# Sliding-window attention with a token mixer: 192 score columns per head and key block, query blocks shifted by 64

## The chip, the cores and the metric

The kernel runs on one core of one Trainium2 chip. The metric is the device time of one execution in microseconds, lower is better. The kernel before took 135.03, 134.73 and 133.62 us in three executions, median 134.73 us.

## What is computed

Attention with a window of 128 keys and a linear distance bias, for 8 batches, 8 heads, 576 positions and head size 64; then a token mixer without a softmax on the 512 joined head columns.

```python
scores = q @ k.T / sqrt(64)                       # B=8, H=8, S=576, D=64
rel    = pos[:, None] - pos[None, :]
mask   = (rel >= 0) & (rel < 128)
scores = where(mask, scores - slope[h] * abs(rel), -1e9)
x      = softmax(scores) @ v                      # joined over heads: [B, 576, 512]
W      = (x @ w_q) @ (x @ w_k).T / sqrt(64)       # w_q, w_k: [512, 64]
out    = relu(W @ x) @ w_out                      # w_out: [512, 512], float32 out
```

A query sees itself and the 127 positions before it. Equally, a key is seen by the 128 queries that begin at its own position.

## The kernel before

**Order of the work.** The program is a graph of small operations, each with its dependencies (`Op`, `Graph.add`). The order in which each engine issues them is written out by hand in one string, ORDER (lines 35 to 119). A word such as `QK2.1.0@PE:2` gives the operation, its engine and its PSUM bank pair (two digits name one bank of a pair); `+11` puts eleven filler matmuls ahead of it. Every engine takes its words strictly in that order, so a word that has to wait holds all later words of its engine. Some PSUM evacuations may stand on ScalarE (ACT) or VectorE (DVE), as the string says.

**Loads.** q, k and v come in by DMAs issued on POOL, one for each block of 128 positions of a batch (Lq, Lk, Lv), with a cast to f16; the last 64 positions of two batches share a load (Lt, Lv with part 4). The first half of batch 0 comes in two loads on SP (Lf). Weights are Lw (w_q, w_k) and Lwo. All of them go through `load` (line 379, the DMA at 383). The buffers hold four batches.

**Attention.** TQ and TT transpose q and k on PE by 64x128 pieces, two row halves (two heads) at a time; ETQ and ETT copy the result to SBUF. For a batch b and a key block g of 128 keys, QK (lines 526 to 548) makes the scores of four heads (u is 0 or 1) with the keys on the partitions and 256 queries in the columns, those from the block's first key on. It is four matmuls, two at a time on two row halves. Key block 3 has 192 such queries, and its last 64 columns take the tail: the last 64 keys with the last 64 queries. EXP (556) makes the exponential of 1024 columns on ACT. MUL (566) multiplies 2048 columns, eight heads, on DVE with a table `bias` that holds the exponential of the distance bias, zero outside the window; `biasl` is the table for block 3. PV (571 to 606) multiplies the result with v, to which a column of ones is joined, so that column 64 of each head is the softmax sum. A query block of 128 takes two key blocks (blocks 1 to 3) or one (block 0), one matmul per head and key block on the full array; part 4 is the tails of two batches on tiles of 64 columns. X (613, 614) takes the reciprocal and scales on DVE.

**Mixer.** XT and EXT transpose x. WQ (669) multiplies x with w_q, which is held twice side by side so that the result stands in both partition halves; EWQ copies it. WK (695 to 701) multiplies x with w_k so that the positions stand on the partitions: four matmuls for each of five blocks of positions; EWK copies it. G sums (x w_k) against x over the positions, MX multiplies the result with x w_q, RM applies ReLU, OUT multiplies with w_out, EO copies to SBUF, DO stores. Up to 26 such output tiles are held in SBUF (HELD). The stores of batches 0 to 5 are issued on POOL behind all loads (lines 850 and 851), those of 6 and 7 on SP.

In the profile most PE work has line 228 (`mm`) or 231 (`tp`, transposes), copies have 235, 237, 241 or 243, so operations are told apart by their tiles: `qkT` QK, `vt,pt` PV, `wk_sb,xT` WK, `xT,wqq_sb` WQ, `x,wkn` G, `wqT,gs` MX, `wout_sb,rm` OUT, `identh,nat` TQ, `identh,natt` TT, `identh,x` XT. The shape of the array (128\*128, 64\*128, 128\*64) stands behind them: rows by columns of one tile.

Of the kernel before, what the change touches and what calls it, by code (L numbers as in the profile page):

```python
# [14 lines left out]
P = 128  # L15
# [12 lines left out]
NPT = 6  # L28
HELD = 26
# [6 lines left out]
zeros@DVE iota@POOL Lf1.0@SP pads@POOL dist@DVE mask@DVE Lf0.0@SP ident@POOL ones2@DVE bias0@ACT  # L36
Lh0.1@POOL idh@DVE ones0@DVE Lh1.1@POOL bias1@ACT Lt0.1@POOL C1.0.1@DVE C1.0.0@ACT Lq1.3@POOL
C0.0.1@ACT biasl1@DVE TQ0.0.1@PE:0+11 C0.0.0@ACT Lk1.3@POOL ETQ0.0.1.0@DVE ETQ0.0.1.1@ACT
TQ0.0.0@PE:1+3 Lt0.0@POOL ETQ0.0.0.1@DVE ETQ0.0.0.0@ACT C0.1.0@ACT ones3@DVE QK0.0.0@PE:0+3/20
Lk1.1@POOL biasl0@DVE QK0.2.0@PE:1 QK0.1.0@PE:2 EXP0.0.0@ACT TQ0.1.0@PE:3 Lk1.2@POOL ETQ0.1.0.0@DVE  # L40
C1.1.0@ACT ETQ0.1.0.1@DVE Lq1.2@POOL EXP0.2.0@ACT TQ0.1.1@PE:0+1 ETQ0.1.1.0@DVE Lk1.0@POOL
EXP0.1.0@ACT ones1@DVE QK0.1.1@PE:1+2/30 ETQ0.1.1.1@DVE QK0.0.1@PE:3 Lq1.1@POOL EXP0.1.1@ACT
QK0.2.1@PE:0+1 TT0@PE:2 Lq1.0@POOL EXP0.2.1@ACT ETT0@DVE ETT1@DVE QK0.3.1@PE:1+1 Lv0.0@POOL
MUL0.1@DVE QK0.3.0@PE:2 EXP0.0.1@ACT Lv0.1@POOL EXP0.3.0@ACT MUL0.2@DVE TQ1.2@PE:0+5 Lw0@POOL
Lv0.2@POOL ETQ1.2@ACT MUL0.0@DVE Lv0.3@POOL EXP0.3.1@ACT QK1.3.1@PE:0+6/30 QK1.3.0@PE:2 QK1.2.0@PE:3
Lk2.0@POOL EXP1.3.1@ACT TQ1.0@PE:1 MUL0.3@DVE Lv0.4@POOL ETQ1.0@ACT PV0.0@PE:0 Lq2.0@POOL X0.0@DVE
EXP1.3.0@ACT PV0.1@PE:1 wqq@DVE Lv1.3@POOL QK1.1.1@PE:0 MUL1.3@DVE QK1.1.0@PE:2 EXP1.1.1@ACT
Lq2.1@POOL EXP1.1.0@ACT X0.1@DVE PV0.2@PE:0 Lv1.2@POOL X0.2@DVE EXP1.2.0@ACT Lw1@POOL QK1.0.0@PE:1
QK1.2.1@PE:2 Lk2.1@POOL MUL1.1@DVE EXP1.2.1@ACT PV0.3@PE:0 Lv1.1@POOL XT0.0@PE:3 EXP1.0.0@ACT
MUL1.2@DVE QK1.0.1@PE:2 Lv1.0@POOL EXT0.0@ACT PV0.4@PE:1 X0.3@DVE Lk2.3@POOL EXP1.0.1@ACT  # L50
WQ0.0@PE:30 X0.4@DVE Lq2.2@POOL XT0.1@PE:0 PV1.3@PE:2 EXT0.1@ACT MUL1.0@DVE Lk2.2@POOL XT0.2@PE:31
XT1.2@PE:10 TQ2.0@PE:0 EXT0.2@ACT EXT1.2@ACT Lq2.3@POOL WK0@PE:31 EWQ0.0@DVE ETQ2.0@ACT X1.3@DVE
PV1.2@PE:1 Lk3.2@POOL WQ0.1@PE:30 EWK0@ACT X1.2@DVE PV1.0@PE:0 Lwo0@POOL EWQ0.1@ACT QK2.0.1@PE:2
X1.0@DVE Lwo3@POOL PV1.1@PE:1 EXP2.0.1@ACT Lwo2@POOL QK2.0.0@PE:3 X1.1@DVE G0@PE:00 EXP2.0.0@ACT
Lwo1@POOL XT1.1@PE:2 EG0@DVE Lt2.1@POOL XT1.0@PE:1 EXT1.1@ACT MUL2.0@DVE MX0.0@PE:0 MX0.1@PE:3
EXT1.0@ACT Lv2.0@POOL TQ2.2@PE:2 RM0.0@ACT WQ1.0@PE:10 ETQ2.2@DVE Lt2.0@POOL WQ1.1@PE:11 RM0.1@ACT
WK1@PE:00 Lq3.0@POOL EWQ1.1@DVE QK2.2.0@PE:2 EWQ1.0@DVE EWK1@ACT QK2.2.1@PE:3 Lq3.3@POOL
EXP2.2.0@ACT MX0.4@PE:1 G1@PE:00 RM0.4@DVE Lk3.3@POOL OUT0.3@PE:01 EXP2.2.1@ACT EG1@DVE Lq3.2@POOL
MX1.4@PE:1 QK2.1.1@PE:2 EO0.3@DVE MX1.1@PE:3 RM1.4@ACT EXP2.1.1@ACT Lk3.0@POOL OUT0.1@PE:00
RM1.1@DVE Lq3.1@POOL TT2@PE:1 EO0.1@ACT QK2.1.0@PE:2 MUL2.2@DVE MX1.0@PE:3 EXP2.1.0@ACT Lk3.1@POOL  # L60
OUT1.4@PE:01 ETT2@DVE RM1.0@ACT Lk4.1@POOL OUT0.0@PE:00 ETT3@DVE MUL2.1@DVE Lv2.1@POOL QK2.3.1@PE:2
EO0.0@ACT QK2.3.0@PE:1 TQ3.2@PE:3 EXP2.3.1@ACT EO1.4@DVE Lv2.4@POOL OUT1.1@PE:00 ETQ3.2@DVE
EXP2.3.0@ACT Lv2.3@POOL PV2.0@PE:2 OUT1.2@PE:01 X2.0@DVE Lv3.3@POOL EO1.1@ACT QK3.3.1@PE:3 EO1.2@ACT
MUL2.3@DVE Lv2.2@POOL TQ3.0@PE:1 EXP3.3.1@ACT QK3.3.0@PE:2 OUT1.3@PE:00 Lq4.0@POOL ETQ3.0@DVE
EXP3.3.0@ACT PV2.1@PE:3 Lk4.0@POOL EO1.3@ACT QK3.1.1@PE:1 X2.1@DVE QK3.1.0@PE:2 Lq4.1@POOL
EXP3.1.1@ACT OUT0.2@PE:01 MUL3.3@DVE Lv3.1@POOL EXP3.1.0@ACT XT2.0@PE:3 QK3.0.1@PE:1 Lq4.2@POOL
EXT2.0@DVE OUT1.0@PE:00 EXP3.0.1@ACT MUL3.1@DVE Lk4.3@POOL PV2.2@PE:2 EO0.2@ACT QK3.2.0@PE:3
Lq4.3@POOL EO1.0@ACT X2.2@DVE PV2.3@PE:1 EXP3.2.0@ACT QK3.2.1@PE:0 Lv3.2@POOL X2.3@DVE PV2.4@PE:2
EXP3.2.1@ACT TQ4.0@PE:3 Lk4.2@POOL X2.4@DVE XT2.1@PE:1 ETQ4.0@ACT WQ2.0@PE:00 Lk5.2@POOL EXT2.1@DVE
XT2.2@PE:01 QK3.0.0@PE:2 EWQ2.0@DVE XT3.2@PE:10 Lv3.0@POOL EXT2.2@ACT QK4.0.0@PE:3 MUL3.2@DVE  # L70
EXP3.0.0@ACT WK2@PE:11 Lt4.1@POOL WQ2.1@PE:00 EXP4.0.0@ACT EWK2@DVE QK4.0.1@PE:2 MUL3.0@DVE
Lk5.3@POOL G2@PE:01 EWQ2.1@ACT EXP4.0.1@ACT Lq5.3@POOL PV3.2@PE:3 EG2@DVE MX2.1@PE:0 X3.2@DVE
EXT3.2@ACT Lq5.2@POOL MX2.0@PE:2 RM2.1@ACT TQ4.2@PE:1 RM2.0@DVE Lq6.3@POOL PV3.3@PE:3 ETQ4.2@ACT
OUT2.3@PE:00 Lt4.0@POOL X3.3@DVE PV3.0@PE:2 EO2.3@ACT QK4.2.0@PE:1 Lv4.1@POOL X3.0@DVE PV3.1@PE:3
EXP4.2.0@ACT Lv4.0@POOL QK4.2.1@PE:0 X3.1@DVE OUT2.0@PE:20 EXP4.2.1@ACT Lq5.1@POOL MUL4.0@DVE
XT3.0@PE:1 EO2.0@ACT QK4.1.1@PE:3 Lk5.1@POOL XT3.1@PE:0 EXT3.0@ACT OUT2.2@PE:21 EXT3.1@DVE
EXP4.1.1@ACT Lq5.0@POOL MUL4.2@DVE QK4.1.0@PE:1 TT4@PE:0 EO2.2@ACT Lk5.0@POOL TQ5.2@PE:3
EXP4.1.0@ACT ETT4@DVE WQ3.1@PE:20 ETQ5.2@DVE Lv4.2@POOL WK3@PE:21 ETT5@ACT EWQ3.1@ACT Lk6.1@POOL
QK4.3.1@PE:1 MUL4.1@DVE EWK3@ACT QK4.3.0@PE:0 MX2.4@PE:3 EXP4.3.1@ACT G3@PE:20 Lv4.3@POOL RM2.4@DVE
WQ3.0@PE:21 EXP4.3.0@ACT Lq6.0@POOL EG3@DVE PV4.0@PE:1 EWQ3.0@DVE MX3.1@PE:3 X4.0@DVE PV4.1@PE:2  # L80
Lq6.2@POOL RM3.1@ACT MX3.0@PE:0 X4.1@DVE TQ5.0@PE:1 Lq6.1@POOL RM3.0@ACT QK5.3.1@PE:3 ETQ5.0@DVE
OUT2.1@PE:20 Lv4.4@POOL EXP5.3.1@ACT Lv5.3@POOL QK5.3.0@PE:0 EO2.1@DVE XT4.0@PE:1 EXP5.3.0@ACT
QK5.0.0@PE:3 EXT4.0@DVE OUT3.1@PE:21 Lk6.0@POOL MUL4.3@DVE EXP5.0.0@ACT Lk6.2@POOL QK5.2.0@PE:1
# [83 lines left out]
def kernel(  # L167
# [51 lines left out]
    def two(bank):  # L219
        return pairs[bank[0]]  # L220

    held = []

    def hold(i):
        held.append(i.ins)

    def mm(*a, **k):
        hold(nc.tensor.matmul(*a, **k))  # L228

    def tp(*a):  # L230
        hold(nc.tensor.transpose(*a))  # L231

# [658 lines left out]
```

## Time and profile before

| | |
|---|---|
| three executions | 133.62, 134.73, 135.03 us |
| span of the profiled execution, first to last instruction | 132.4 us |
| mean granted TensorE clock | 0.997 |
| PE, DVE, ACT, POOL busy | 121.7, 112.3, 112.9, 109.6 us |
| PE busy in 0 to 30 us | 10.00 of 10: 8.09, 8.43, 7.54 |
| HBM read, written | 29.62 MB, 9.44 MB |

The executions in the first row include what lies around the span. In the profile an operation's duration is its own, while successive matmuls overlap: the distance from one start to the next says what PE spends, not the sum of durations. A row of PE's timeline merges matmuls of the same tiles that follow one another.

### The profile page before, as it was taken

Reading aid. Unit: us, or ns where it says so; the run is one execution under the profiler, and the core shown is the slowest. Engines: PE = TensorE matmul, PEld = TensorE weight load, DVE = VectorE, ACT = ScalarE, POOL = GpSimd, SP = SyncE. Lnnn points to the kernel's source line nnn. Section 1 sums busy time; section 2 is a strip of 40 time slices with the busy share of each in tenths; the row PEclk is TensorE's granted clock in tenths of the full one; section 3 lists DMA queues with packets and bytes.
Section 4 is the critical chain, followed back from the end, with each engine's and each line's share of the span. In section 5 each row is a group of like instructions: output and inputs, shape, how many; then the busy total and the mean of one; then the engine's idle time right before and its main releaser. Section 6 shows DMA issues by size and latency. Waiting matters only on the chain.

```text
span 132.4 us, 5423 instructions
## 1 busy us (share of the span) xinstructions
PE 121.7 (92%) x2349; PEld 77.6 (59%) x2349; DVE 112.3 (85%) x206; ACT 112.9 (85%) x163; POOL 109.6 (83%) x147
## 2 busy tenths in 40 slices
PE   6988795888999999999999999999999999999970
PEld 2343364676774565767677667567567656863430
DVE  6776958997978999999999999999999999982530
ACT  5999779986999999999999999999999897554730
POOL 7999879999999999999999999999968509790000
PEclk9999999999999999999999999999999999999998
DMA  3999999999999999999999999999999936999775
GB/s 119 275 148 155 157 158 152 149 151 149 189 156 158 156 155 153 157 153 154 156 154 156 153 152 153 156 157 152 157 212 376 374 125 228 334 303 367 285 211 185
DMA packets 110663, 25.12 MB, mean 190 GB/s; under 512 B 104816, under 2 KB 107888, under 8 KB 110640
## 3 DMA queue, kind: packets, MB, share of 16 engines
q0 software_dynamic: 108128, 21.37, 178.4%
q1 hardware_dynamic: 2512, 3.41, 7.5%
q8 instruction: 18, 0.29, 0.8%
q14 instruction: 5, 0.04, 0.1%
HBM read 29.62 MB, written 9.44 MB: 295 GB/s over the span
## 4 chain that ended last, share of the span: by engine, by line
PE 77%; ACT 7%; POOL 6%; DMA 6%; issue 1%; POOLq 0%; ACTq 0%
PE pair L228 67%; PE pair L231 10%; DMA nat<-in_q_dram 6%; ACT pt L556 5%; POOL nat L383 4%; ACT qkT L241 1%; POOL natt L383 1%; ACT osb L235 1%; POOL ident masks.py:199 0%; POOL ident masks.py:197 0%; POOL xT L339 0%; POOL xT L340 0%; POOL wint L311 0%; ACTq L556 0%; POOLq L311 0%
## 5 line engine op out<-in xcount | busy, mean ns | idle before, releaser
L556 ACT ACTIVATE pt<-pair 128x1024 f16<-128x1024 f32 x64 | 63.2, 1033 | 1.6 <-PE pair L228 1.3
L383 POOL DMA_DIRECT2D vt<-in_v_dram x32 | 31.7, 1138 | 0.9 <-DMA nat<-in_q_dram 0.9
L228 PE MATMUL pair<-wout_sb,rm 128*128 128x512 f16 (+1 forms) x132 | 32.4, 374 | 0.0
L383 POOL DMA_DIRECT2D nat<-in_k_dram x29 | 29.2, 1059 | 0.5 <-DVE pt L566 0.5
L383 POOL DMA_DIRECT2D nat<-in_q_dram x29 | 29.0, 1058 | 0.1
L566 DVE TENSOR_TENSOR pt<-pt,bias 128x2048 f16<-128x2048 f16 x24 | 29.0, 1217 | 0.0
L228 PE MATMUL pair<-vt,pt 128*128 128x65 f16 (+1 forms) x512 | 21.4, 194 | 2.9 <-ACT pt L556 1.6
L228 PE MATMUL pair<-qkT 64*128 64x256 f16 (+2 forms) x320 | 23.3, 250 | 0.8 <-DVE qkT L243 0.3
L228 PEld LDWEIGHTS <-pt 128*128 128x128 f16 (+1 forms) x576 | 19.0, 100 | 8.1 <-issue 6.0
L614 DVE TENSOR_TENSOR x<-pair,inv 128x512 f16<-128x512 f32 x32 | 22.1, 692 | 1.1
L235 ACT COPY osb<-pair 128x512 f32<-128x512 f32 (+1 forms) x29 | 16.7, 585 | 4.3 <-PE pair L228 4.0
L797 POOL DMA_DIRECT2D out_dram<-osb x24 | 13.5, 604 | 6.4 <-ACT osb L235 4.7
L228 PEld LDWEIGHTS <-rm 128*128 128x128 f16 x132 | 10.9, 97 | 11.9 <-issue 1.9
L228 PEld LDWEIGHTS <-qkT 64*128 64x128 f16 x320 | 10.8, 94 | 8.3 <-issue 4.7
L731 ACT ACTIVATE rm<-pair 128x1024 f16<-128x1024 f32 (+1 forms) x12 | 11.3, 956 | 1.4 <-PE pair L228 1.2
L228 PE MATMUL pair<-fill 128*128 128x512 f16 x33 | 10.6, 453 | 1.7 <-DVE fill L364 1.2
L243 DVE COPY qkT<-pair 128x2048 f16<-128x2048 f16 (+1 forms) x12 | 10.4, 884 | 1.5 <-PE pair L231 1.5
L231 PEld LDWEIGHTS <-nat 64*128 64x128 f16 x512 | 9.1, 95 | 4.0 <-ACT nat L235 1.3
L231 PE MATMUL pair<-identh,nat 64*128 64x64 f16 x512 | 10.4, 190 | 1.1 <-DMA nat<-in_q_dram 0.7
L566 DVE TENSOR_TENSOR pt<-pt,biasl 128x2048 f16<-128x2048 f16 x8 | 9.7, 1219 | 1.6 <-ACT pt L556 1.6
L228 PE MATMUL pair<-xT,wqq_sb 128*128 128x256 f16 (+1 forms) x64 | 10.4, 287 | 0.0
L241 ACT COPY qkT<-pair 128x1024 f32<-128x1024 f32 (+1 forms) x10 | 8.2, 834 | 1.5 <-PE pair L231 1.4
(66 smaller groups left out, 161.8 us busy)
## 6 DMA issues: line engine op xcount, KB each, us to landing
out_dram<-osb POOLq DMA_DIRECT2D x24, 256.0 KB, 4.7
vt<-in_v_dram POOLq DMA_DIRECT2D x32, 128.0 KB, 6.0
nat<-in_q_dram POOLq DMA_DIRECT2D x28, 128.0 KB, 5.7
nat<-in_k_dram POOLq DMA_DIRECT2D x28, 128.0 KB, 5.8
out_dram<-osb SPq DMA_DIRECT2D x7, 256.0 KB, 2.6
out_dram<-osb POOLq DMA_DIRECT2D x6, 128.0 KB, 4.3
nat<-in_k_dram SPq DMA_DIRECT2D x1, 512.0 KB, 3.8
nat<-in_q_dram SPq DMA_DIRECT2D x1, 512.0 KB, 4.7
```

The costliest lines, as they stand in the source:

```text
L228: hold(nc.tensor.matmul(*a, **k))
L231: hold(nc.tensor.transpose(*a))
L235: hold(nc.scalar.copy(out_ap, in_ap))
L241: hold(nc.scalar.copy(out_ap.bitcast(FP32), in_ap.bitcast(FP32)))
L243: hold(nc.vector.tensor_copy(out=out_ap, in_=in_ap))
L383: op = add(kind, b, part, (eng,), deps, lambda o: q.dma_start(out=dst, in_=src), size=size)
L556: nc.scalar.activation(out=pt[:, u, 0:1024], in_=two(s.bank).rearrange("p e c -> p (e c)"), func=AF.Exp, scale=SCALE)
L566: nc.vector.tensor_tensor(out=pt[:, :, 0:1024], in0=pt[:, :, 0:1024], in1=bt, op=ALU.mult)
L614: nc.vector.tensor_tensor(out=x.rearrange("p (g h d) -> p g h d", g=2, h=4), in0=pxv[:, :, :, 0:64], in1=inv.unsqueeze(3).broadcast_to([P, ...
L731: hold(nc.scalar.activation(out=out_ap, in_=in_ap, func=AF.Relu, scale=WSCALE))
L797: q.dma_start(out=out[b, P * st:P * st + P, c], in_=osb)
```

## The change

**Scores by half key blocks.** A key block of 128 keys is treated as two halves of 64. Each half needs the 191 queries that begin at its own first key, so 192 columns serve it (KW). The scores of the lower half stand in PSUM partitions 0 to 63, for queries 128g to 128g+191. Those of the upper half stand in partitions 64 to 127: columns 64 to 191 are queries 128g+64 to 128g+191, columns 0 to 63 are the next 64 queries (in block 3: the tail keys and queries). So columns 64 to 191 have the same queries in both halves, and columns 0 to 63 have other queries in each. EXP covers 768 columns, MUL 1536. A QK unit is twelve matmuls on 64x64 tiles.

**Query blocks shifted by 64.** Block qt now covers queries 64+128qt to 64+128qt+127, the tail block the first 64 queries of two batches. PV gives the main product: one key block, columns 64 to 191, full array. The side products come from columns 0 to 63 on 64x64 tiles: the lower key half of block qt+1 for the block's upper 64 queries, the upper key half of block qt-1 for its lower 64 (PW; in blocks 1 and 2 PS and PW). PS and PW of one query block write the two PSUM banks crosswise from two row halves. Between them stands T, an empty instruction on SP that waits for PS, and PW waits for T (SYNC). The reciprocal becomes an operation of its own, R.

**w_q and w_k in one product.** The two weights stand side by side, so WQ gives x w_q in partitions 0 to 63 and x w_k in 64 to 127. EWD copies x w_q to the other half. WKT transposes x w_k by five transposes in place of WK's twenty products; the last batch keeps WK.

**Loads wait (AHEAD).** Each load on POOL waits until the load six before it has landed. Stores no longer wait for all loads; ORDER is written anew, with 296 words on PE instead of 248, 37 fillers instead of 33, the weight loads first, and some stores ahead of the last v loads.

```diff
+SYNC = True
+KW = 192
+AHEAD = 6
...
+    def after(i, j):
+        tc.add_manual_dep(i, j.name, mybir.DependencyInfo(
+            mybir.DependencyClass.Sync, mybir.DependencyReason.DATA), reason="kept behind")
+    def behind(i, op):
+        for j in op.insts[-2:]:
+            after(i, j)
...
-        op = add(kind, b, part, (eng,), deps, lambda o: q.dma_start(out=dst, in_=src), size=size)
+        def go(o):
+            i = q.dma_start(out=dst, in_=src).ins
+            if eng == "POOL":
+                going.append(i)
+                if len(going) > AHEAD:
+                    after(i, going[-1 - AHEAD])
+        op = add(kind, b, part, (eng,), deps, go, size=size)
...
-        return [(g, P * g, 256, 0)] if g < 3 else [(3, 384, 192, 0), (4, 512, 64, 192)]
+    def segs(g, c):
+        if c == 0:
+            return [(P * g, P * g, KW, 0)]
+        k0 = P * g + 64
+        return [(k0, k0, P, 64), (k0, P * g + KW, 64, 0) if g < 3 else (512, 512, 64, 0)]
...
+                for e, c, i in ((0, 0, 0), (1, 0, 0), (0, 1, 0), (1, 1, 0), (0, 1, 1), (1, 1, 1)):
+                    r = slice(64 * e, 64 * e + 64)
+                    for k0, q0, n, at in segs(g, c)[i:i + 1]:
+                        mm(ps[64 * c:64 * c + 64, e, KW * a + at:KW * a + at + n],
+                           t[r, 1, hp, k0:k0 + 64], t[r, 0, hp, q0:q0 + n], start=True, stop=True)
...
-            nc.vector.tensor_tensor(out=pt[:, :, 0:1024], in0=pt[:, :, 0:1024], in1=bt, op=ALU.mult)
+            nc.vector.tensor_tensor(out=pt, in0=pt, in1=bt, op=ALU.mult)
...
+        def part(g, r, i, u, px, vals, **k):
+            h, at, cols = spot(i, u)
+            rows = slice(64 * r, 64 * r + 64)
+            mm(px[:, u, cols], g[rows, at, 0:64], vals[rows, h, 0:65], **k)
+        def em_main(o):
+            px = out(o)
+            for i in range(4):
+                for u in range(2):
+                    h, at, cols = spot(i, u)
+                    mm(px[:, u, cols], tile_of(b, qt)[:, at, 64:KW], vt_s[b % NV][qt][:, h, 0:65],
+                       start=(i == 0), stop=False)
...
+        def em_both(swap):
+            def go(o):
+                px = out(o)
+                for i in range(4):
+                    for r in range(2):
+                        u, kb = r ^ swap, qt + 1 - 2 * r
+                        part(tile_of(b, kb), r, i, u, px[64 * (1 - r):64 * (1 - r) + 64], vt_s[b % NV][kb],
+                             start=False, stop=(i == 3))
+                if swap and SYNC:
+                    behind(held[0], o.deps[0])
+            return go
...
+                f = add("PS", b, qt, PE, [p, *side, ones], em_both(0), mode=3)
+                w = f
+                if SYNC:
+                    def mark(o):
+                        hold(nc.sync.nop())
+                        behind(held[0], f)
+                    w = add("T", b, qt, SP, [f], mark)
+                w = add("PW", b, qt, PE, [w, f], em_both(1), mode=3, size=qt)
...
-                mm(pw[:, 0:n], wqq_sb[:, c, :], xT_s[b % 2][:, c, lo:lo + n], start=(c == 0), stop=(c == 3))
+                mm(pw[:, 0:n], wqk_sb[:, c].rearrange("p e j -> p (e j)"), xT_s[b % 2][:, c, lo:lo + n],
+                   start=(c == 0), stop=(c == 3))
...
+            cps(o.eng, wqd_s[b % 2][64:128, :], wqk_s[b % 2][0:64, :])
+        ewd[b] = add("EWD", b, "", EV, [ewq[b, 0], ewq[b, 1], pads, *mxd.get(b - 2, [])], em)
...
+            def emt(o, ts=ts):
+                for i in ts:
+                    flip(oneh(o.bank)[:, 64 * i:64 * i + 64], wqk_s[b % 2][64:128, at[i]:at[i] + P], 1)
...
-                q.dma_start(out=out[b, P * st:P * st + P, c], in_=osb)
+                q.dma_start(out=out[b, 64 + P * st:64 + P * st + P, c], in_=osb)
...
-    for d in late:
-        d.deps += issues
```

462 lines of the change are left out of this document (239 added, 223 removed).

## The prediction

> **What bounds the kernel now.** I read the page first (busy slices, chain that ended last), then the chain in order of time, PE's own waits, and PE's timeline, because a busy digit of PE says little where matmuls overlap.
>
> ```profile
> span 132.4 us, 5423 instructions
> PE   6988795888999999999999999999999999999970
> PE 77%; ACT 7%; POOL 6%; DMA 6%; issue 1%; POOLq 0%; ACTq 0%
> ```
> ```profile
> 26.85 1.24 PE pair L228 x35
> ...
> 115.84 11.51 PE pair L228 x102
> 127.35 0.02 issue
> ```
> ```profile
> PE pair L228 <- ACT pt L556: 2.1, 4, 0.8
> PE pair L228 <- DVE fill L364: 1.2, 1, 1.2
> PE pair L231 <- DMA nat<-in_q_dram: 0.7, 1, 0.7
> ```
> From 26.85 to 127.35 us the chain never leaves PE. PE's longest wait in total is 2.1 us, for the exponentials. So there are three stretches: a start of 26.9 us in which loads and ScalarE decide, 100.5 us of PE, and 5.0 us in which the last copies and stores leave. Is PE filled or only pipelined? The timeline tells, by the distance from one group's start to the next one's:
>
> ```profile
> 85.58 0.74 PE L228 MATMUL pair<-wk_sb,xT 128*128 128x64 f16 x20
> 86.16 0.42 PE L228 MATMUL pair<-vt,pt 128*128 128x65 f16 x8
> 86.51 0.39 PE L228 MATMUL pair<-qkT 64*128 64x256 f16 x4
> 86.83 0.66 PE L228 MATMUL pair<-vt,pt 128*128 128x65 f16 x16
> 87.43 0.39 PE L228 MATMUL pair<-qkT 64*128 64x256 f16 x4
> 87.75 0.63 PE L228 MATMUL pair<-x,wkn 128*64 128x256 f16 x8
> ...
> 88.42 0.41 PE L231 MATMUL pair<-identh,natt 64*128 64x64 f16 x16
> 88.66 0.38 PE L228 MATMUL pair<-qkT 64*128 64x256 f16 x4
> ```
> ```profile
> 65.83 0.39 PE L228 MATMUL pair<-qkT 64*128 64x256 f16 x4
> 66.05 0.43 PE L231 MATMUL pair<-identh,x 64*128 64x64 f16 x16
> ```
> Every distance recurs, whatever the engines beside it do. A score unit followed by work of the same tile shape takes 0.22 to 0.23 us (65.83 to 66.05), and 0.32 when the shape of the array changes behind it (86.51 to 86.83, 87.43 to 87.75). So a change of shape costs 0.10 us. PV of one key block is 0.25 (0.35 less 0.10), PV of two 0.50, the twenty w_k products 0.58, sixteen transposes on two row halves 0.24, which is 30 ns for a pair. PE has hardly a hole to fill: **only less PE work, or an earlier start, shortens the middle.** VectorE and ScalarE are near full too, but they are not what PE waits for.
>
> **The change, part by part, against the span of 132.4 us.** The three executions took 133.62, 134.73 and 135.03 us, so 2.3 us lie around the span at the median; I keep that.
>
> **Exponentials and mask.** Each EXP shrinks from 1024 to 768 columns, each MUL from 2048 to 1536.
>
> ```profile
> L556 ACT ACTIVATE pt<-pair 128x1024 f16<-128x1024 f32 x64 | 63.2, 1033 | 1.6 <-PE pair L228 1.3
> L566 DVE TENSOR_TENSOR pt<-pt,bias 128x2048 f16<-128x2048 f16 x24 | 29.0, 1217 | 0.0
> ```
> ```profile
> L731 ACT ACTIVATE rm<-pair 128x1024 f16<-128x1024 f32 x10 | 10.1, 1026 | 1.4 <-PE pair L228 1.2
> L731 ACT ACTIVATE rm<-pair 128x512 f16<-128x512 f32 x2 | 1.2, 602 | 0.0
> ```
> ```profile
> L243 DVE COPY qkT<-pair 128x2048 f16<-128x2048 f16 x7 | 8.5, 1217 | 0.2 <-PE pair L231 0.2
> L243 DVE COPY xT<-pair 128x1024 f16<-128x1024 f16 x8 | 5.5, 684 | 0.2 <-PE pair L231 0.2
> ```
> ReLU gives ScalarE's slope, (1026 - 602)/512 = 0.83 ns a column, so an EXP falls by 212 ns and 64 of them by 13.6 us. The copies give VectorE's, (1217 - 684)/1024 = 0.52, so a MUL falls by 266 ns and 32 of them by 8.5 us. Eight new copies EWD (640 columns moved as 320 words) cost some 0.45 us each. On the path this is nearly nothing: PE's whole wait for EXP is 2.1 us, and in the start loads also decide. **I take -0.5, bounds -2.1 and 0.** The mixer now also waits for EWD; in the last batch OUT6.1 and OUT6.3 stand between on PE, some 0.9 us each, against two copies of 0.45. Without them it would cost 0.45 once.
>
> **Scores.** A unit was four matmuls of 256 columns in two row halves. It becomes twelve on 64x64 tiles: per column half of the array 192, or 128 and 64, columns for each of two head pairs. A pair of 256 columns takes 0.115 us, 0.45 ns a column. If the two column halves run side by side, 2 x 192 columns take 0.17; if one after the other, 2 x 384 take 0.34. No row shows 64x64 tiles. The nearest one, tiles of 64 columns on all rows, does run two at a time:
>
> ```profile
> 80.79 0.22 PE L228 MATMUL pair<-vt,pt 128*64 128x65 f16 x2
> ...
> 81.29 0.20 PE L228 MATMUL pair<-vtl,pt 128*64 128x65 f16 x2
> 81.42 0.39 PE L228 MATMUL pair<-qkT 64*128 64x256 f16 x4
> ```
> 32 matmuls in 0.53 us (0.63 less a change of shape) are 33 ns a pair, about what one alone would need (PV: 0.25/8 = 31 ns). I take 0.185, nearer to side by side, with 15 ns for more instructions: 64 x (0.185 - 0.230) = **-2.9 us, bounds -3.8 and +7.0.**
> The Trainium skill speaks against this (TensorEngine Tiling (Array Packing), Feature Incompatibilities): column tiling does without the fast weight load. By its page TensorE: Matmul & The Clock Gate (LDWEIGHTS) 64 columns then load in 53 ns; an estimate from that, with twelve loads in turn, is 0.64 us a unit and 26 us in all. The row above, with 17 ns for a load and its matmul together, does not bear it out for 64-column tiles; no row shows it for 64x64.
>
> **PV.** 448 matmuls on the full array and 128 in the tails become 256 on the full array and 528 on 64x64 tiles. Before: 8 x 0.25 + 24 x 0.50 + 4 x 0.53 = 16.1. After: 32 x 0.25 = 8.0; of the small ones, 64 (first block) run alone at 33 ns, 2.1, and 464 in pairs at 33 ns, 7.7; together 17.8. **+1.7, bounds -2 (four at a time) and +9 (each alone).**
>
> **w_k.** Seven batches lose their twenty products (0.58) for five transposes of the product that w_q and w_k now share; five at 30 ns are 0.15. **-3.0.** All five in one row half may run one by one; at 30 ns each that is counted, and in pairs the gain grows by 0.5 (bounds -3.5 and -2.5).
>
> **Changes of shape.** In the PE order as written out there are 132 before and 137 after: **+0.5.**
>
> **A wait over SP (T).** In sixteen query blocks the second half of the side products (PW) waits for an SP instruction that waits for the first half (PS). Behind PW stands all of PE's queue, and R and X of that block on VectorE.
>
> ```profile
> L228 PE MATMUL pair<-vt,pt 128*64 128x65 f16 x64 | 2.6, 197 | 0.5 <-ACT pt L556 0.5
> ```
> ```profile
> 119.73 0.59 ACT L235 COPY osb<-pair 128x512 f32<-128x512 f32 x1 [0.23 <-PE pair L228]
> ```
> ```profile
> 120.34 3.98 SPq L797 DMA_DIRECT2D out_dram<-osb  x4
> ```
> The copy ends at 120.32 and SP starts at 120.34: a hop to SP is 0.02 to 0.05. A last matmul's 0.2, two hops and the SP instruction make a trip of some 0.3. Three trips (0.1, 0.2, 1.1) have nothing between, 0.9 us. Three (4.2, 5.1, 5.2) have one score unit, 0.1 each. The other ten have two units, or other side products, and cost about 0.02. **+1.4, bounds 0 (hidden by load waits of the start) and +8 (a trip of 0.8).**
>
> **Loads wait (AHEAD).** Each POOL load waits until the sixth before it has landed.
>
> ```profile
> 16.77 0.88 POOL L383 DMA_DIRECT2D vt<-in_v_dram  x1 [0.89 <-DMA nat<-in_q_dram]
> 18.18 0.88 POOL L383 DMA_DIRECT2D nat<-in_k_dram  x1 [0.53 <-DVE pt L566]
> ...
> 88.22 7.48 POOL L383 DMA_DIRECT2D vt<-in_v_dram  x8
> 95.15 2.20 POOL L797 DMA_DIRECT2D out_dram<-osb  x3
> ```
> ```profile
> nat<-in_q_dram POOLq DMA_DIRECT2D x3, 128.0 KB, 7.2
> ```
> ```profile
> nat<-in_q_dram POOLq DMA_DIRECT2D x2, 128.0 KB, 5.3
> ```
> ```profile
> nat<-in_q_dram POOLq DMA_DIRECT2D x3, 128.0 KB, 6.0
> ```
> POOL issues one load per (95.15 - 88.22)/8 = 0.87 us, so six take 5.2, while issue to landing takes 7.2 (issued in 10 to 15 us), 5.3 (20 to 25) and 6.0 (75 to 85). The new wait will therefore hold POOL. But POOL paused 1.4 us at 16 to 18 and landing time fell by about as much, 7.2 to 5.3: what is waited out is a queue of the transfers, not their length. So the landings should keep their pace. They matter, for the plan runs close to them. Lk7.3 is the 97th load: 2.6 + 90 x 0.87 + 6 short ones at 0.57 + 0.6 of memsets puts its issue at 85, its landing at 90 to 91. Behind TQ7.2, which needs it, the order has 31.1 us of PE work at the prices above (19 OUT 15.7, six WQ 2.9, nine PV 2.3, 14 MX 2.0, the rest 8.2) and 31 changes of shape: PE can't end before 124.2 to 125.2. Without any wait for it PE would end at 127.35 less the sum of the terms so far, 2.8, at 124.6. **I charge +0.8 for loads, bounds 0 and +8 (first rival).** Six output stores now stand ahead of Lv7.1 on POOL; at 0.6 each that is 3.6 us, covered, since only 18 us of PE work follow PV7.1.
>
> **Nothing on the path:** fewer memsets (VectorE idles in the start anyway), three iotas for one with the pads moved behind, R apart from X on the same engine, output rows shifted by 64. The last store still follows the last OUT by a copy and a transfer.
>
> **Sum:** -0.5 - 2.9 + 1.7 - 3.0 + 0.5 + 1.4 + 0.8 = -2.0. The span goes to 130.4, the time to **132.7 us**, 1.5% faster. A measurement of this kernel tells about 1% from no change.
>
> **Rivals.**
> *The load wait sets the pace (slower).* If 6.0 us are the length of a transfer, a load can start every 6.0/6 = 1.0 us instead of 0.87, and Lk7.3 lands 12 us later, at 102; with 34 us behind it PE ends at 136 and the time is 144. For it: landing exceeds 5.2 in every window. Against: the pause at 16.77. It decides from a pace of 0.91.
> *Column halves one after the other (slower).* A unit of 0.34 us adds 64 x 0.155 = 9.9: 142.6. It costs more than 1% over before from 0.24 us a unit. For: twelve loads and twelve matmuls per unit, never seen here. Against: the pairs at 33 ns.
> *Longer trips over SP (no change).* At 0.5 the three bare trips cost 1.5, the three others 0.9, the ten 1.5: +2.5, 135.2. For: sixteen round trips that did not exist. Against: 0.02 to SP.
> *The start shortens as well (faster).* PE gets the whole 2.1 of ScalarE's waits and the loads hold nothing: 130.3. Against: the plan's closeness to Lk7.3.
>
> **Chances.** Forecast 0.42, shorter start 0.10, longer trips or another loss of like size 0.26, column halves 0.14, load wait 0.08. Faster by over 1%: 0.42 + 0.10 = 0.52; within: 0.26; slower: 0.14 + 0.08 = 0.22. The range runs from 129.5, a little under the shorter start, to 138, which takes in trips near 0.7 and a unit up to 0.27; outside stay the load wait, most of the column case and a little below, 0.2. The forecast's own range is 131 to 133.4.
>
> **What would show it.** Score units on 64x64 tiles 0.17 to 0.20 us from start to start where PE is dense, and PE still the chain from some 26 us on. EXP near 820 ns, MUL near 950, both engines with holes. Gaps of 0.3 us ahead of PW0.1, PW0.2 and PW1.1 and nearly none later. POOL with gaps put down to DMA, landings still 0.85 us apart and the last q/k load down by 91. The forecast is wrong if score units pass 0.24, if PE waits on DMA for more than 2 us after 30 us, or if ACT or DVE takes over the chain.

## The result, and the profile after

The changed kernel takes 143.58 us (median of four executions, 141.01 to 144.31), the kernel before on the same chip 134.41 (four, 133.62 to 135.03): a ratio of **1.0565, interval 1.0466 to 1.0664**. It is slower by 5.7%, where 1.5% faster was forecast. The profiled execution took 143.03 us; its span is 141.3, that of before 132.4. All ratios below compare undisturbed executions alone, while a median takes in all of them; the profiled one of e1 ran at a granted clock of 0.85 almost throughout, so it serves for counting stops and not for times.

The page of the changed kernel: the span, the busy tenths of PE, the granted clock, and the chain by engine.

```profile
span 141.3 us, 6529 instructions
PE   6997579889689999979999998979769999999950
PEclk9999969999999999999999999999999999999999
PE 42%; DMA 24%; POOL 21%; issue 6%; DVE 2%; ACT 0%; POOLq 0%; DVEq 0%
```

PE had the chain with 77%; now DMA and POOL hold 45% of it, and a class that was 1% has grown to 6%: "issue", time in which the engine waited for nothing that the profile shows. PE's own waits in the changed kernel (us in total, times, longest):

```profile
PE pair L241 <- issue: 2.5, 3, 0.9
PE pair L238 <- issue: 1.6, 2, 1.2
PE pair L241 <- DMA nat<-in_q_dram: 1.6, 2, 1.3
...
PE pair L238 <- DMA vt<-in_v_dram: 0.9, 1, 0.9
...
PE pair L241 <- DMA natt<-in_q_dram: 0.2, 1, 0.2
```

Two things have grown: 2.7 us for loads (0.7 before), and 4.1 us for nothing (0.5 before). The chain in order of time shows where (start, us, what):

```profile
82.62 5.08 DMA nat<-in_q_dram
...
94.17 0.82 issue
...
98.73 0.92 issue
...
104.64 1.21 issue
```

PE's timeline around the second of these stops:

```profile
98.39 0.35 PE L241 MATMUL pair<-identh,x 64*128 64x64 f16 x9
99.65 0.31 PE L241 MATMUL pair<-identh,x 64*128 64x64 f16 x7 [0.92 <-issue]
```

XT5.1 is sixteen transposes of tiles that are all there. Nine run, TensorE stands still for about a microsecond, seven follow. No engine, semaphore or load explains a stop **inside** an operation. What is left is the instruction stream itself, and the page's list of DMA queues has it: the queue "instruction", packets and MB, before

```profile
q8 instruction: 18, 0.29, 0.8%
```

and in the changed kernel

```profile
q8 instruction: 22, 0.36, 1.0%
```

A packet is 16 KB (0.36 MB in 22). Number TensorE's instructions as the trace has them: matmuls, weight loads and some ten others. There are 4708 for 18 packets before and 5821 for 22 in the changed kernel, about 256 to a packet. In the seventeen traces of this study the rows of PE put 56 stops of more than 0.3 us down to "issue". All 56 stand between the instructions 256n + 193 and 256n + 195, and end 1.2 to 1.8 us after an instruction packet has come in. So a stop of this kind is TensorE at the end of one packet, waiting for the next. (The rows count idle time of PE, whose busy time holds the tail of each matmul; measured from the end of the columns, as in the numbers from the trace below, a stop is up to 0.2 us longer.)

The loads. POOL's issues between 60 and 90 us, before (out, in, count, KB, median us from issue to landing):

```profile
nat<-in_q_dram POOLq DMA_DIRECT2D x11, 128.0 KB, 5.8
vt<-in_v_dram POOLq DMA_DIRECT2D x11, 128.0 KB, 6.0
nat<-in_k_dram POOLq DMA_DIRECT2D x10, 128.0 KB, 6.0
```

and in the changed kernel:

```profile
nat<-in_k_dram POOLq DMA_DIRECT2D x11, 128.0 KB, 4.8
nat<-in_q_dram POOLq DMA_DIRECT2D x10, 128.0 KB, 4.8
vt<-in_v_dram POOLq DMA_DIRECT2D x8, 128.0 KB, 4.7
```

With the few tail loads, which are not shown, it is 37 loads in 30 us before and 32 after, 0.81 against 0.94 us a load. Landing got shorter, as the prediction had it, but not short enough to keep the pace.

### The profile page after: what moved, and what is told of

It reads as the page before. It is cut to its first block, busy times and chain, and to the rows that moved or that the text cites. A ratio compares the mean times of both kernels' runs of the same rounds, so it can differ in the third digit from the quotient of the medians.

```text
span 141.3 us, 6529 instructions
## 1 busy us (share of the span) xinstructions
PE 122.8 (87%) x2904; PEld 81.4 (58%) x2904; DVE 103.8 (73%) x186; ACT 100.9 (71%) x167; POOL 110.4 (78%) x150
## 4 chain that ended last, share of the span: by engine, by line
PE 42%; DMA 24%; POOL 21%; issue 6%; DVE 2%; ACT 0%; POOLq 0%; DVEq 0%
PE pair L238 36%; POOL nat L391 16%; DMA vt<-in_v_dram 8%; DMA nat<-in_k_dram 8%; PE pair L241 7%; DMA natt<-in_q_dram 5%; DMA nat<-in_q_dram 4%; POOL wout_sb L391 1%; POOL wqk_sb L391 1%; POOL vtl L391 1%; DVE pt L580 1%; POOL natt L391 1%; DVE xtl L685 0%; DVE x L685 0%; DVE wqd L247 0%
## 5 line engine op out<-in xcount | busy, mean ns | idle before, releaser
L570 ACT ACTIVATE pt<-pair 128x768 f16<-128x768 f32 x64 | 48.9, 814 | 12.7 <-PE pair L238 12.2
L238 PE MATMUL pair<-vt,pt 64*64 64x65 f16 (+1 forms) x704 | 27.5, 194 | 2.8 <-issue 1.2
L238 PEld LDWEIGHTS <-pt 64*64 64x64 f16 (+1 forms) x768 | 23.5, 104 | 9.0 <-issue 2.9
L238 PE MATMUL pair<-qkT 64*64 64x128 f16 (+2 forms) x768 | 22.3, 224 | 3.5 <-ACT qkT L245 1.0
L580 DVE TENSOR_TENSOR pt<-pt,bias 128x1536 f16<-128x1536 f16 x24 | 22.5, 949 | 2.1 <-ACT pt L570 2.1
L238 PEld LDWEIGHTS <-qkT 64*64 64x64 f16 x768 | 16.0, 107 | 9.1 <-issue 5.3
L238 PE MATMUL pair<-fill 128*128 128x512 f16 (+1 forms) x53 | 13.1, 378 | 1.2 <-DVE fill L371 1.2
L247 DVE COPY osb<-pair 128x512 f32<-128x512 f32 (+1 forms) x16 | 10.6, 667 | 2.8 <-PE pair L238 2.6
L682 DVE RECIPROCAL inv<-pair 128x8 f32<-128x8 f32 x36 | 6.9, 201 | 7.3 <-PE pair L238 6.1
L827 DVE TENSOR_SCALAR rm<-pair 128x1024 f16<-128x1024 f32 (+1 forms) x8 | 8.6, 1084 | 2.6 <-PE pair L238 2.5
```

The lines of the kernel that those rows point to most:

```text
L238: return hold(nc.tensor.matmul(*a, **k))
L247: hold(nc.vector.tensor_copy(out=out_ap, in_=in_ap))
L570: nc.scalar.activation(out=pt[:, 4 * u:4 * u + 4, :].rearrange("p (e a) c -> p e (a c)", e=2), in_=two(s.bank)[:, :, 0:2 * KW], func=AF.Ex ...
L580: nc.vector.tensor_tensor(out=pt, in0=pt, in1=bt, op=ALU.mult)
L827: hold(nc.vector.tensor_scalar(out=out_ap, in0=in_ap, scalar1=0.0, scalar2=WSCALE, op0=ALU.max, op1=ALU.mult))
```

## The experiments

**First theories.** A: the wait of loads sets the pace (the first rival of the prediction). B: the new order of loads and stores on POOL starves TensorE. C: the new pieces and the trips over SP cost more than summed. Four runs were made before the stops were understood; each edit is one line or a move.

*e1, the changed kernel without the wait.*

```diff
-AHEAD = 6
+AHEAD = 1000
```


> The changed kernel with AHEAD set to 1000, so that no load waits for an earlier one; nothing else is changed. Theory A (the wait for the sixth load before sets the pace): the forecast's sum holds once it is gone, corrected for score units of 0.204 us instead of 0.185, 132 to 136 us, last v load down by 103 us instead of 113.6. Theory B (the new order of loads and stores, with the weights first and six stores among the last loads, starves PE): 140 us or more. Theory C (PE's new pieces and the trips over SP cost more than summed): 139 us or more, with PE dense.

146.73 us (144.24 to 149.97), ratio 1.078 (1.0654 to 1.0906): without the wait the kernel is **slower still**. The last k load now lands at 91.0 us, as the prediction had it, and TensorE hardly waits for loads (0.8 us, once); it waits for nothing instead:

```profile
PE pair L241 <- issue: 4.0, 4, 1.7
PE pair L238 <- issue: 2.7, 3, 1.6
```

A alone is refuted.

*e2, the kernel before with the wait of six,* by the same lines in its load helper.


> The kernel before with the wait alone: each POOL load waits until the load six before it has landed. Theory A: 140 to 147 us, last v load down by 109 to 114 us instead of 100.6. Theories B and C, which hold the wait for harmless: 133 to 136 us, only issue to landing shorter.

139.59 us, ratio 1.0405 (1.033 to 1.0479), just under A's 140 to 147: the wait alone costs 5.0 us there, and PE's waits say for what:

```profile
PE pair L229 <- DMA vt<-in_v_dram: 3.4, 5, 0.9
...
PE pair L232 <- DMA natt<-in_q_dram: 1.1, 2, 0.8
PE pair L232 <- DMA nat<-in_q_dram: 0.9, 3, 0.5
```

No row with "issue" is left. So A is right for the kernel before, and wrong for the changed one.

*e3, the wait at eight loads* (AHEAD = 8).


> The changed kernel with AHEAD 8 instead of 6. Theory A in the form of a lost reserve (landings come late by 1 to 2 us now and then, and with six in flight POOL stands until they are down): eight in flight allow 8 x 0.87 = 6.9 us of landing time, so most of the loss is gone, within 1.5 us of the run without any wait. If a wait costs by itself, by the 0.28 us from landing to the next issue, at each load: still 139 us or more. Theories B and C: as the changed kernel, 143.

147.3 us (144.85 to 149.57), ratio 1.0812 (1.0691 to 1.0933), as slow as e1. TensorE's stops come to 9.5 us:

```profile
PE pair L238 <- issue: 4.9, 6, 1.9
PE pair L241 <- issue: 4.6, 5, 1.6
```

*e4, six stores behind the last loads:* DO3.1, DO0.2, DO1.3, DO1.0, DO2.2 and DO0.0 moved behind Lv7.1 in the order.


> The changed kernel, with AHEAD 6, and with the six stores that stand among the last v loads on POOL moved behind the last load. Theory B: 2 us or more faster, 141 or less, because the last v loads land 4 us earlier. Theory A: within 1.5 us of the changed kernel, since PE has 18 us of work behind PV7.1 and the q and k loads, which come before, set the end.

142.56 us, ratio 1.0622 (1.0529 to 1.0714): no difference from the changed kernel. B falls.

**The theory that took their place.** D: TensorE's instructions come in packets of 256, the next is asked for when TensorE enters the one before, and it is held up by the loads. Rival E: the stops belong to the 64x64 tiles or to the new waits. More instructions without any 64x64 tile, and fewer with the same tiles, tell them apart.

*e5, the kernel before with more instructions.*

```diff
-                        mm(ps[:, e, 256 * a + c0:256 * a + c0 + wd],
-                                         t[r, 1, hp, P * kb:P * kb + P],
-                                         t[r, 0, hp, q0:q0 + wd], start=True, stop=True)
+                        for x in range(0, wd, P if wd == 256 else wd):
+                            w = min(P if wd == 256 else wd, wd - x)
+                            mm(ps[:, e, 256 * a + c0 + x:256 * a + c0 + x + w],
+                               t[r, 1, hp, P * kb:P * kb + P],
+                               t[r, 0, hp, q0 + x:q0 + x + w], start=True, stop=True)
...
-            for db in range(4):
...
-                mm(one(o.bank)[:, 0:n], lt, wout_sb[:, db, c], start=(db == 0), stop=(db == 3))
+            for x in range(0, n, P):
+                for db in range(4):
...
+                    mm(one(o.bank)[:, x:x + P], lt, wout_sb[:, db, c.start + x:c.start + x + P],
+                       start=(db == 0), stop=(db == 3))
```


> The kernel before with the same arithmetic in more TensorE instructions: a score piece of 256 columns goes out as two of 128, an OUT product of 512 as four of 128; 588 more matmuls with their weight loads, as many as the changed kernel has. Theory D (new): TensorE's instructions come by DMA in packets of 256, those packets queue among the loads' packets, and TensorE stops for 0.5 to 2 us, in the middle of an operation and released by nothing, when it uses a packet up before the next has come. D expects such stops here, 4 us or more in the waits put down to issue (0.5 in the kernel before), and 139 to 145 us. Theory E (rival): the stops belong to 64x64 tiles, or to the waits the change adds; then none here beyond 1 us, only the pieces' own cost of 1 to 2 us: 135.5 to 137.

139.31 us (137.04 to 141.53), 4.8 more than before by the medians. The four executions lie far apart at granted clocks of 0.98 to 1.00, so no ratio is given, and the fastest stands only 2.5 above before; the time alone does not tell D from E. The trace has 2969 matmuls to 2349, 620 more and not 588. There is no tile of 64x64 in it, and the stops are there:

```profile
PE pair L228 <- issue: 2.9, 4, 1.3
PE pair L231 <- issue: 2.7, 3, 1.2
```

E falls.

*e6, the changed kernel without the wait, q and k from whole rows* (other data, as many bytes).

```diff
-                                          t[b, :, P * n:P * n + P, :].transpose([1, 0, 2]))
+                                          nat_s[b % NNAT][j][:, n].rearrange("p h d -> p (h d)"), whole(t, b, n))
```


> The changed kernel without the wait of loads, its q and k loads taking as many bytes from whole rows of 2 KB instead of 256-byte pieces (so other data of the same tensor), which takes away half of all DMA packets. D: TensorE's instruction packets come quickly, the stops released by nothing fall from the 8 to 10 us of the two runs with little or no wait to under 2, and the time is 130 to 135. E (64x64 tiles stop by themselves): stops of 8 us or more stay, 143 to 147. C (new pieces cost more than the sum has): stops go but units stay dear, 136 to 142.

145.4 us, ratio 1.0788 (1.0712 to 1.0865). D's expectation **failed**: the page counts 61260 DMA packets instead of some 111400, and the stops are hardly fewer than without the wait.

```profile
PE pair L238 <- issue: 4.6, 5, 2.9
PE pair L241 <- issue: 1.6, 3, 0.7
```

So the number of the loads' packets is not what holds up an instruction packet here.

*e7, the changed kernel without the wait, 192 matmuls fewer.*

```diff
-        return [(k0, k0, P, 64), (k0, P * g + KW, 64, 0) if g < 3 else (512, 512, 64, 0)]
+        return [(k0, k0, KW, 0)] if g < 3 else [(k0, k0, P, 64), (512, 512, 64, 0)]
```


> The changed kernel without the wait of loads; in the first three key blocks the two pieces of 128 and 64 score columns of the second column half are one of 192, so these columns stand turned by 64 in the tile and the result is another one. 192 matmuls and 192 weight loads fewer, the same columns. D: fewer stops, 4 to 7 us instead of 8 to 10, and with 0.6 us for the shorter units 140 to 143. E: stops stay, 143.5 to 147.

142.5 us, ratio 1.0496 (1.0424 to 1.0569), stops of 4.2 us in PE's waits, as D has it: 4.2 us under e1 by the medians, 3.6 by the executions that the ratios compare.

*e8, the kernel before with whole rows,* the control for e6.


> The kernel before with its q and k loads from whole rows of 2 KB (other data of the same tensor), as the control for the changed kernel with such loads. D: little to gain, since it has one stop of 0.7 us: 131 to 134.5; the changed kernel with such loads then differs from it by the terms of the prediction's sum without the wait, that is -2.8 us, give or take 2. E: the same time here, and the changed kernel 9 us or more above it.

134.15 us, ratio 0.9958 (0.992 to 0.9997), as D has it for this kernel; the second half, that the changed kernel would then stand under it, failed with e6.

*e9 and e10, the changed kernel with score units of four products, without and with the wait.*

```diff
-                for e, c, i in ((0, 0, 0), (1, 0, 0), (0, 1, 0), (1, 1, 0), (0, 1, 1), (1, 1, 1)):
...
-                    for k0, q0, n, at in segs(g, c)[i:i + 1]:
-                        mm(ps[64 * c:64 * c + 64, e, KW * a + at:KW * a + at + n],
-                           t[r, 1, hp, k0:k0 + 64], t[r, 0, hp, q0:q0 + n], start=True, stop=True)
+                for e in range(2):
                     r = slice(64 * e, 64 * e + 64)
...
+                    mm(ps[:, e, KW * a:KW * a + KW], t[r, 1, hp, P * g:P * g + P],
+                       t[r, 0, hp, P * g:P * g + KW], start=True, stop=True)
```


> The changed kernel without the wait of loads, its score units as four products of 128 keys and 192 columns in two row halves (as before the change, 64 columns fewer): 512 matmuls and 512 weight loads fewer than the changed kernel, nearly the number of the kernel before. Left out: the other queries of the second key half, so 64 of its columns hold other scores. Theory D (instruction packets) expects stops released by nothing of at most 2 us instead of 8 to 10, and, as the rest of the prediction's sum then holds, 132 to 136 us. Rival E (the side products on 64x64 tiles, the trips or the order itself cost the time): 139 or more.

> The same kernel with the wait of loads (six). With few instructions the wait has only its cost: theory A with D expects 3 to 6 us over the one without it, 136 to 141, with TensorE waiting for DMA and no stops. If the wait shortens the stops and costs nothing else, it is as fast as the one without.

e9: 137.85 us, ratio 1.025 (1.0199 to 1.0301). The stops are gone, one row is left:

```profile
PE pair L241 <- issue: 0.2, 1, 0.2
```

and with them 8.9 us of e1's time by the medians, 6.8 by the executions that the ratios compare; but 137.85 lies above D's 132 to 136, so 2 us or more are lost elsewhere (below). e10: 139.69 us, ratio 1.0388 (1.034 to 1.0436). The wait costs 1.8 us here, less than A's 3 to 6, and is paid in waits for loads as expected; one stop of 0.4 us is left.

*e11, the kernel before with the more instructions of e5 and the wait of e2.*


> The kernel before with both additions, the 588 more matmuls and the wait of loads. Alone they cost 4.8 and 5.0 us. D expects less than their sum, since fewer loads in flight let the instruction packets through sooner: 140 to 142.5, with stops of under 3 us where the run without the wait had 5.6. If the two are independent: 144 to 145.

140.41 us, ratio 1.0422 (1.0346 to 1.0498), where 4.8 and 5.0 would add up to 144.3 (2.5 and 5.0 to 142.0). PE's waits have no "issue" any more, and loads instead:

```profile
PE pair L229 <- DMA vt<-in_v_dram: 2.0, 3, 1.2
...
PE pair L232 <- DMA natt<-in_q_dram: 0.9, 1, 0.9
```

Both families side by side, by the executions that the ratios compare (us, medians):

```
                              no wait     wait of six
before                        134.5       139.6   (e2)
before, 620 matmuls more      137.0 (e5)  140.2   (e11)
changed, 512 matmuls fewer    137.9 (e9)  139.7   (e10)
changed                       144.7 (e1)  142.0
```

More instructions cost 2.5 and 6.8 us without the wait, 0.6 and 2.3 with it. The wait costs 5.1 and 1.8 us where instructions are few, 3.2 where they are many in the kernel before, and **gives 2.7** in the changed one. Neither edit has a price by itself. The 137.0 is one execution; with the median of e5's four, 139.3, the 2.5 would be 4.8 and the 3.2 would be 0.9.

*e12, the shared w_q and w_k product alone,* in three batches of the kernel before (G and MX moved behind the longer chain).

```diff
+            if b in SH:
+                t = add("WKT", b, name, PE, [idh, pads, ewq[b, 0], ewq[b, 1]], emt, banks=1, mode=1)
+            else:
+                t = add("WK", b, name, PE, [wts[1], pads, *[ext[b, i] for i in ts]], emk, banks=1, size=len(ts))
```


> One part alone: the kernel before with w_q and w_k in one product and five transposes for the twenty w_k products in batches 1, 4 and 5 (with the copy that this needs), 45 matmuls fewer; everything else as before, two output buffers fewer. The prediction's price, 0.43 us a batch, gives 1.3 us less: 132.5 to 133.8. Rival: the chain product, copy, transposes, copy is one copy longer, and TensorE waits for it: 134.5 or more.

136.46 us, ratio 1.0147 (1.0109 to 1.0186): the rival. PE waits for copies of that chain, which it did not before:

```profile
PE pair L227 <- DVE gs L236: 1.4, 2, 1.2
...
PE pair L227 <- ACT wkn L240: 0.4, 1, 0.4
```

It says nothing against the price of the product; it shows that the price is only had with an order laid for the longer chain. No version tried here beats the kernel before by more than a measurement can tell.

**What stayed open, and two more runs.** e6 spoke against the loads as what holds the packets up, the effect of the wait spoke for them. If it is the loads' bytes in flight, halving those must help (D); if the packets are slow by themselves, not (F).

*e13, e1 with half the bytes in the loads of batches 5 to 7 (four of the eight heads; the others keep older data); e14, e5 with the same.*

```diff
+    def some(b):
+        return H if b <= NNAT else H // 2
...
-                                          nat_s[b % NNAT][j][:, n],
-                                          t[b, :, P * n:P * n + P, :].transpose([1, 0, 2]))
+                                          nat_s[b % NNAT][j][:, n, 0:some(b)],
+                                          t[b, 0:some(b), P * n:P * n + P, :].transpose([1, 0, 2]))
```


> The changed kernel without the wait of loads, where the q, k and v loads of batches 5 to 7 bring four of the eight heads (the other heads keep the data of the batch four before). TensorE's instructions are all there. D, with the packets held up by the bytes of the loads in flight: the stops after 63 us, 6.9 us in the run without the wait, fall under 2.5 us, the packets start 1.0 to 2.0 us after TensorE enters the packet before (2.6 there), and the time is 138 to 142. Theory F (the packets are slow whatever the loads do): stops after 63 us stay over 5 us, 144 or more.

> The kernel before with 588 more matmuls, its loads of batches 5 to 7 halved in the same way. D: the five stops after 63 us, 5.0 us there, fall under 2 us, and of the 4.8 us that the matmuls cost at least 2.5 are given back: 134.5 to 137. F: stops and time stay, 138.5 to 140.

e14: 136.09 us, ratio 1.0111 (1.0051 to 1.0172). Of the stops only those ahead of the halved loads are left, and 3.2 of the 4.8 us are back by the medians (1.0 of 2.5 against e5's fastest execution, so the evidence is the stops more than the time):

```profile
PE pair L231 <- issue: 0.7, 2, 0.4
...
PE pair L228 <- issue: 0.3, 1, 0.3
```

e13: 142.62 us, ratio 1.0515 (1.0424 to 1.0605), 4.1 under e1 by the medians and 3.1 by the executions that the ratios compare. Its stops after 63 us come to 3.7, not to the under 2.5 that D expected, with 6.9 in e1. F falls; in the changed kernel its densest stretch still stops with half the bytes. How long a packet takes to start after TensorE has entered the one before, median between 63 us and the last load, worked out from the DMA records:

```
                             us      stops in the whole trace (number, us)
before                       2.4     1, 0.7
before + wait (e2)           1.5     0
before + matmuls (e5)        3.0     7, 6.7
  + wait (e11)               2.0     0
  + half loads (e14)         1.6     3, 1.5
changed                      2.3     5, 4.9
  no wait (e1)               2.6     8, 8.3
  no wait, half loads (e13)  1.9     5, 5.0
  no wait, whole rows (e6)   2.6     9, 7.9
```

Each median stands on 5 to 10 packets that spread by 1 us or more. Of the other traces, e3, e7 and e9, with the wait at eight loads or none, have 2.6, 2.5 and 2.8; e4, e10 and e15, with the wait at six, have 1.9, 2.0 and 2.2; e8 and e12, without a wait, have 2.0 and 1.8 and don't fit. All packets with whole loads taken together, by what was in flight at their start, are clearer:

```
                               packets   us, median
nothing moving for 2 us        11        0.7
4 to 7 stores, no load         35        1.2
5 loads, no store              75        1.8
6 loads, no store              65        2.2
7 loads, no store              65        2.5
8 loads, no store              10        2.5
```

(The first two rows take in e13 and e14.) So a packet's delay grows with what is in flight. It is not the loads alone: the stops of e3 at 109.3 us, e6 at 104.2 and e13 at 101.1 follow packets that started with no load and five or six output stores in flight, after 2.8, 1.5 and 1.9 us. That it is bytes and not DMA packets is argued: e6 halved the packets alone and changed nothing against e1, e13 and e14 halved both; but e8, with half the packets of the kernel before, has 2.0 to its 2.4. The transfer adds 0.9 to 1.7, and at a stop the first use stands 1.2 to 1.8 behind it. That a packet is asked for when TensorE enters the one before is read from the 0.5 to 0.85 us of the first row, and was not tried by itself.

*e15, the last eight steps in the order before.* OUT7.4 ahead of the halves of OUT7.3; some copies change their engine with it.

```diff
-MX7.4@PE:3 MX7.1@PE:0 EO7.2@DVE OUT7.3.1@PE:21 RM7.1@ACT DO6.3@SP OUT7.3.0@PE:10 EO7.3.1@DVE
...
-DO7.1@SP EO7.0@ACT DO7.0@SP OUT7.4@PE:31 EO6.2@ACT DO6.2@SP EO7.4@ACT DO7.4@SP
+MX7.4@PE:3 MX7.1@PE:0 EO7.2@DVE OUT7.0@PE:10 RM7.4@DVE RM7.1@ACT DO6.3@SP OUT7.1@PE:11 EO7.0@ACT
...
+EO7.4@DVE OUT7.3.0@PE:10 EO7.3.1@ACT DO7.4@SP DO7.3.1@SP EO7.3.0@ACT DO7.3.0@SP
```


> The changed kernel, its last eight steps in the order before: the two half products of OUT7.3 last, the whole row product OUT7.4 with its two stores ahead of them. In the changed kernel 5.5 us lie between the last matmul's start and the end, before 4.5. If that is the order's doing, 0.7 to 1.2 us come back: 142.0 to 143.2 beside 143.6; if not, no difference.

141.24 us, ratio 1.0471 (1.0419 to 1.0523), an interval that overlaps the changed kernel's. Its trace has 5.5 us from the last matmul's start to the end, as the changed kernel has. So the expectation about the order failed, and whether this run is faster at all stays unclear.

## Why the prediction was wrong, point by point

**The price list held, nearly.** EXP and MUL, us and mean ns in the changed kernel:

```profile
L570 ACT ACTIVATE pt<-pair 128x768 f16<-128x768 f32 x64 | 48.9, 814 | 12.7 <-PE pair L238 12.2
L580 DVE TENSOR_TENSOR pt<-pt,bias 128x1536 f16<-128x1536 f16 x24 | 22.5, 949 | 2.1 <-ACT pt L570 2.1
```

820 and 950 were forecast. The score unit on 64x64 tiles:

```profile
92.65 0.54 PE L238 MATMUL pair<-qkT 64*64 64x192 f16 x24
93.12 0.32 PE L241 MATMUL pair<-identh,xtl 64*128 64x64 f16 x4
```

Two units and a change of shape in 0.47 us are 0.185 each, the number taken. Over all dense places the distance has a median of 0.192 ahead of the same shape (0.229 before) and 0.299 ahead of another (0.325 before): about -2.1 instead of -2.9. The column halves run side by side; that rival, and the estimate of 0.64 us a unit that was worked out from the Trainium skill, are refuted. By the same distances PV costs 1.0 more (1.7 forecast) and w_k 3.4 less (3.0). The changes of shape were under-priced: the 132 and 137 that were counted are in the traces, but with the fillers of the start, and without them it is 115 before and 133 after, +1.8 instead of +0.5. Together -2.7 where -3.7 was summed. The SP trips were right: 0.26 us at PW0.1, PW0.2 and PW1.1, 0.8 in all, and 0.1 or less later.

**The step that failed first is the loads' +0.8.** Its argument was that what the wait holds back is a queue of the transfers and not their length, "so the landings should keep their pace". Landing fell from 6.0 to 4.8 us, but six loads at POOL's 0.87 are 5.2, so 0.4 us are left in reserve: one late landing and POOL stands. The pace went to 0.94, the last k load landed at 98.2 instead of 90 to 91, and TensorE's waits for loads grew by 2.0 us, 0.6 of them in the first 30. Alone, in e2, the same wait costs 5.0.

**The larger miss has no term in the sum: instruction packets.** The prediction priced PE by the time of a matmul and asked only whether 64x64 matmuls pair up. It never asked at what rate instructions arrive. Matmuls in the windows from 80 to 100 us, PE busy us and count first, before

```profile
80.00:100.00 20.00, 20.00 (x460) 13.35 (x459) 19.74 (x32) 19.52 (x28) 18.84 (x25) 1.00 2.33 173
```

and in the changed kernel:

```profile
80.00:100.00 20.00, 17.85 (x562) 13.61 (x562) 16.87 (x31) 16.59 (x26) 18.42 (x23) 1.00 2.19 141
```

With a weight load to each, 256 instructions last 5.6 us before and 4.6 after; of the 4.6, stops of 1.7 us in this window are 0.4, so without them it would be 4.2. A packet needs 2.3 until it starts, 0.9 to come and 1.4 to be used, 4.6 us, and 4.9 without the wait (2.6). The kernel before stood a little on the safe side of this, the changed one would use its instructions faster than they come, and stops. Its stops are 4.9 us to 0.7.

The Trainium skill describes the blocks (Runtime: NRT & Kernel Launch, Instruction fetch mechanics): refills of 256 instructions, the next fetched while the current one runs, and it calls the fetch hidden, since an engine dispatches more slowly than the fill. The blocks agree with the 16 KB packets here; that the fetch is hidden does not, by up to 9.5 us of stops in e3.

**The account of the span,** 8.9 us: the price list -2.7, packets +4.2, loads +2.0, trips +0.8, and 1.1 behind the last matmul (5.5 us from its start to the end, 4.4 before), which the prediction put at nothing. That is 5.4; the 3.5 that remain were not divided by an experiment. By e9 they are hardly the packets' or the wait's: it has neither the wait nor a stop above 0.2 us, and its span of 135.4 is still 3.0 us above before, where about the same price list, trips and end would put it 0.8 under. So theory C, that more is lost than was summed, is not refuted for this part. Part of it lies in the start: TensorE reaches its first transpose of x at 27.25 us (25.50 before), in the first 30 us PE waits 2.6 us for copies of q and k (1.3 before), though less for exponentials (0.7 to 2.1), and the granted clock falls (table of windows, the last three columns are clock, DMA share, GB/s).

```profile
10.00:20.00 10.00, 6.52 (x197) 4.30 (x195) 7.26 (x11) 8.20 (x12) 8.43 (x10) 0.92 2.29 147
20.00:30.00 10.00, 8.86 (x253) 6.46 (x252) 7.40 (x15) 5.42 (x9) 9.30 (x12) 0.91 2.22 141
```

For 3.4 us, from 18.5 to 21.9, TensorE ran at half its clock; before, both windows have 1.00. e9, with the same order of work, has 6.8 us at half clock. That an idle window of some 3.4 us halves the clock is a rule of the Trainium skill (TensorE: Matmul & The Clock Gate, What's actually happening). The length agrees with this trace; but the 3.4 us before 18.5 were thin and not idle, with PE busy for 1.2 of them. What the start costs by itself was not measured, and where the 1.1 us behind the last matmul come from is open after e15.

**The rivals.** The load wait as a rival was put at 144 us with Lk7.3 at 102 and a chance of 0.08. The time came out at 143.6, and yet the rival is not what happened: it lands at 98.2, and without the wait the kernel gets slower. A right number is no proof of its mechanism. None of the three signs by which the forecast called itself wrong came: score units stayed at 0.19 us, ACT and DVE hold 2% of the chain, and PE waits on DMA for 1.4 us after 30 us, as the other 1.3 us for q loads lie in the start:

```profile
PE pair L238 <- DMA vt<-in_v_dram: 0.9, 1, 0.9
...
PE pair L241 <- DMA nat<-in_q_dram: 0.3, 1, 0.3
...
PE pair L241 <- DMA natt<-in_q_dram: 0.2, 1, 0.2
```

What did tell against it are two things that it expected and that failed to come: the last q/k load down by 91, and PE as the chain from 26 us on. No sign looked at the row "issue", though PE's waits of the kernel before had it:

```profile
PE pair L228 <- issue: 0.5, 1, 0.5
```

It is one stop, in PV1.0 at 32 us, at the same place in the stream as all the others.

## What to carry to other kernels

Count TensorE's instructions per microsecond as well as their time: with loads in flight this kernel got 256 of them, 128 matmuls with their weight loads, per 4.6 to 4.9 us by the sum above. By that estimate a matmul below some 37 ns on average is paid by its instructions. A wait that thins the loads costs what it delays and gives what it lets through, so price it together with the change that it comes with. Stops inside an operation with nothing to release them are the sign; look for them, and for the count of instruction packets, before splitting matmuls into smaller tiles.

## What the runs showed of the hardware that was not expected

All 56 stops of more than 0.3 us that PE's rows put down to "issue" stood at the same place in TensorE's stream, at instruction 256n + 193 to 195, and ended 1.2 to 1.8 us after a packet's end. A packet started 0.5 to 0.85 us after TensorE entered the one before when nothing else moved, and after a median of 1.2 with output stores alone, 1.8 with five loads in flight, 2.2 with six and 2.5 with seven. Halving the number of DMA packets at the same bytes changed nothing in the changed kernel (2.6 and 2.6) and gave 2.0 for 2.4 in the one before; halving bytes and packets together gave 1.6 for 3.0 and 1.9 for 2.6.
